# Combining the first group's tokens during the last batch, and loading weight blocks four ahead

## The chip, the cores and the metric

The kernel runs on one core of one Trainium2 chip. The time is device microseconds (us) for one launch. Before the change the median of 3 runs is 1449.72 us (1448.48 to 1450.27). One execution was also recorded by the hardware profiler; it took 1448.71 us, of which 1446.8 us are the span of the trace.

## The reference

Eight batches of 576 tokens with 512 channels go through three layers in a row:

```
x  = q_s @ (k_s^T @ v)          per head (8 heads of 64); q_s: softmax over the head's channels,
                                k_s: softmax over the tokens
h  = gelu(x @ w_in);  u, v = the two halves of h (512 each)
x  = x + (u * (w_sg @ layernorm(v) + b_sg)) @ w_out
u  = x + (x^T @ U @ V)^T        rank 32, over the tokens
out = u + relu(u @ w_ch1) @ w_ch2        w_ch1 is 512 x 2048, w_ch2 is 2048 x 512
```

The large weights arrive as float64, and everything must be accurate to about single precision, so that each product is made of three: every operand is split into a high and a low part (names end in h and l), and high*high, high*low and low*high are added.

## The kernel before

**Batches.** The loop over b = 0..7 (line 1049) does one batch at a time. Its stages on TensorE are Vh (`emit_Vh`, tile pv: the v half of x @ w_in, then layer norm), Uh (`emit_Uh`, tile pu: the u half, four pieces f), S (`emit_S`, tile pS: the product with w_sg, four pieces f, then `split_G`, which makes gh on ScalarE and gl on VectorE), y (`emit_y`, tile py: the product with w_out; every py adds over all four gh and gl). What is left of batch b (`emit_yT`, `emit_U`, `emit_PV`: the rank-32 layer, result yt stored to u2d in DRAM) is done during Vh of batch b + 1. Beside a batch's products the attention of the next batch is prepared (q and k in softmax, tiles qt, kt). pu, pS, py and others share three PSUM buffers, so that a product can begin when the one three earlier was read out; a pu is read out by ScalarE's `ut<-pu` (line 616).

**Steps.** The last layer works on the tokens of all batches in 5 groups of 480 (the last of 384) columns, by a scheme that needs 7 products where 8 blocks would be multiplied. Per group there are 28 steps for w_ch1 and 28 for w_ch2; a step s is 12 matmuls. It needs combinations of token blocks (`u_prep`: 11 VectorE operations and 7 ScalarE copies uh for each of two halves kc, 22 and 14 in all) and a combination of weight blocks, wd, which `fetch` reads from DRAM into a ring of five tiles wu. Group 0 is the tokens of batches 0 and 1, whose u2d has long been written when the last batch runs. Steps 0 to 6 are interleaved with the end of the last batch (line 1166); steps 7 and on run in the loop of line 1209.

**Conversions.** wd is made from the float64 weights by pieces in the queue `pieces`: 16 sets, each of 4 `Block` pieces (load stg, clamp on VectorE, exponent f on ScalarE, two bit operations on VectorE) and 7 `Factor` pieces (sometimes an add f<-f,f, a copy chw on ScalarE, its low part on GpSimd, a store wd<-chw to DRAM). `more(n)` pushes n pieces one stage further; the table `spread` says how many at each place of a batch, and every step calls `more(3)`. At most three pieces are in `loaded`, so a load is issued at most three rounds before VectorE's clamp asks for it. A chw tile has three buffers; a buffer is free when its store has landed.

**Order of the work.** TensorE runs in the order in which the program is written. In batches 0 to 6 VectorE does too, in batch 7 ScalarE, and from step 7 on ScalarE, VectorE, GpSimd and SyncE; where an engine isn't held, a list scheduler orders it when the kernel is built. All loads and stores but the token loads of u_prep and the residuals are issued by SyncE, one after another: one that waits holds up those behind it.

Of the kernel before, what the change touches and what calls it, by code (L numbers as in the profile page):

```python
# [22 lines left out]
def fused_kernel(tc, q, k, v, w_in, g_ln, w_sgT, b_sg, w_out, U, V, w_ch1, w_ch2, outT):  # L23
    nc = tc.nc
    B, S, C = q.shape
    P = 128
# [57 lines left out]
    wi_p, close_wi = opened("wi_p", side="left")  # L84
# [19 lines left out]
    wi_h = wi_p.tile([P, NC, 2 * F], F32R, name="wi_h")  # L104
    wi_l = wi_p.tile([P, NC, 2 * F], F32R, name="wi_l")
# [208 lines left out]
    class Factor(Conv):  # L314
# [12 lines left out]
        def merge(self):  # L327
# [10 lines left out]
            self.hl = stgp.tile([P, 2, CW], F32R, tag="chw", name="chw")  # L338
# [215 lines left out]
    def emit_Vh(b, t):  # L554
        xh, xl, xr, _ = x_t[b]
        pv = ps2.tile([P, 1024], F32, tag="big", name="pv")[:, 0:F]
        cols = slice(F, 2 * F)
        for kc in range(NC):
            if t < NT:
                a, l = xh[:, kc, t * P : (t + 1) * P], xl[:, kc, t * P : (t + 1) * P]  # L560
                mm(pv, a, wi_h[:, kc, cols], kc == 0, False)
                mm(pv, a, wi_l[:, kc, cols], False, False)
                mm(pv, l, wi_h[:, kc, cols], False, kc == NC - 1)
            else:
                a = xr[:, kc].rearrange("p j r -> p (j r)")
                mm(pv, a, wi_h[:, kc, cols], kc == 0, False)
                mm(pv, a, wi_l[:, kc, cols], False, kc == NC - 1)
# [40 lines left out]
    def emit_Uh(b, f):  # L608
# [5 lines left out]
        for kc in range(NC):  # L614
            prod(pu, wi_h[:, kc, fs], wi_l[:, kc, fs], xh[:, kc], xl[:, kc], kc == 0, kc == NC - 1)
# [359 lines left out]
    mid = ((0, 0, 1, 0, 1), (0, 0, 0, 1), (1, 1, 1, 1), (1, 1, 1, 1))  # L975
# [310 lines left out]
```

## Time and profile before

| | |
|---|---|
| median of 3 runs | 1449.72 us |
| profiled execution | 1448.71 us |
| its span | 1446.8 us |
| TensorE busy | 1314.5 us (91%) |
| VectorE, ScalarE, GpSimd busy | 1058.1, 605.7, 479.4 us |
| mean granted TensorE clock | 0.97 |

Batches 1 to 6 take the same time each. Batch 7 follows from 568.3 us, step 7 begins at 697.6, step 28 at 777.5. A slice of the page's second part is 36.2 us long, so the last batch and the first 28 steps are the slices 16 to 22, counted from 1.

### The profile page before, as it was taken

The numbers are of one execution on the slowest core, as the hardware profiler recorded it, in microseconds if no ns is written. First come the engines' busy times: TensorE is split into PE (matmuls) and PEld (weight loads), VectorE is DVE, ScalarE is ACT, GpSimd is POOL, SyncE is SP. The second block draws the span as 40 slices with busy tenths as digits, with TensorE's granted clock in tenths as the row PEclk, the third lists the DMA queues.
The fourth block names the chain that finished last, engine by engine and source line by source line (L and its number), as shares of the span: only waits on it lengthen the run. The fifth ranks groups of instructions, "written<-read, shape, count | busy, mean of one in ns | idle before, by whom it ended". The sixth has DMA issues, their size and how long they took to land.

```text
span 1446.8 us, 20595 instructions
## 1 busy us (share of the span) xinstructions
PE 1314.5 (91%) x7576; PEld 1156.8 (80%) x7576; DVE 1058.1 (73%) x1489; ACT 605.7 (42%) x969; POOL 479.4 (33%) x516
## 2 busy tenths in 40 slices
PE   4689999999999999938868899999999999999998
PEld 3478898989898989827757788878887888779988
DVE  7778878787878786576657894698549864986594
ACT  4665747575756564433224341134113411242132
POOL 5953626262626262642332130023101210131013
PEclk9899999999999999958988999999999999999999
DMA  7515242424242420447987777668766876688776
GB/s 239 159 35 158 99 114 99 114 98 114 99 114 99 113 99 30 165 139 239 305 287 271 249 251 230 202 230 268 235 203 198 295 240 203 206 259 283 254 239 207
DMA packets 116339, 269.16 MB, mean 186 GB/s; under 512 B 11856, under 2 KB 39312, under 8 KB 116240
## 3 DMA queue, kind: packets, MB, share of 16 engines
q1 hardware_dynamic: 108816, 239.54, 50.9%
q0 software_dynamic: 7424, 28.32, 5.8%
q8 instruction: 60, 0.98, 0.3%
q14 instruction: 39, 0.32, 0.1%
HBM read 219.58 MB, written 48.23 MB: 185 GB/s over the span
## 4 chain that ended last, share of the span: by engine, by line
PE 49%; DVE 26%; ACT 10%; DMA 7%; issue 6%; POOL 2%; SPq 1%; ACTq 0%; POOLq 0%; DVEq 0%
PE mm L49 32%; PE py L49 7%; PE pS L49 3%; DVE h L787 3%; DMA stg<-in_w_ch_dram 2%; DVE ol L787 2%; DVE f L177 2%; PE pv L49 2%; DVE ol L52 2%; DMA wd<-chw 2%; DVE qt L52 2%; DVE km L52 2%; DVE f L178 1%; DVE ul L52 1%; DVE bst L581 1%
## 5 line engine op out<-in xcount | busy, mean ns | idle before, releaser
L49 PE MATMUL mm<-oh,wu 128*128 128x480 f32 (+1 forms) x1120 | 326.7, 373 | 8.6 <-ACT oh L58 5.9
L49 PE MATMUL mm<-uh,wu 128*128 128x480 f32 (+1 forms) x1064 | 315.4, 378 | 15.1 <-DVE h L52 9.7
L49 PEld LDWEIGHTS mm<-oh,wu 128*128 128x128 f32 x1120 | 207.9, 188 | 40.3 <-ACT oh L58 12.7
L49 PEld LDWEIGHTS mm<-uh,wu 128*128 128x128 f32 x1064 | 202.0, 192 | 44.9 <-DVE h L52 11.0
L49 PE MATMUL mm<-ol,wu 128*128 128x480 f32 (+1 forms) x560 | 211.8, 378 | 11.7 <-DVE ol L52 9.3
L49 PE MATMUL mm<-ul,wu 128*128 128x480 f32 (+1 forms) x532 | 200.9, 378 | 0.0
L52 POOL TENSOR_TENSOR res<-res,u 128x960 f32<-128x960 f32 (+1 forms) x20 | 53.6, 2681 | 375.5 <-ACT u L58 311.8
L52 DVE TENSOR_TENSOR h<-mm,u 128x960 f32<-128x960 f32 (+1 forms) x76 | 84.5, 1112 | 87.9 <-PE mm L49 87.9
L49 PEld LDWEIGHTS mm<-ol,wu 128*128 128x128 f32 x560 | 105.4, 188 | 35.7 <-DVE ol L52 18.3
L52 POOL TENSOR_TENSOR chw<-f,chw 128x256 fp32r<-128x256 f32 x112 | 90.3, 813 | 130.4 <-ACT chw L58 129.2
L916 ACT ACTIVATE h<-h 128x960 f32<-128x960 f32 (+1 forms) x20 | 19.5, 974 | 261.2 <-DVE h L52 261.2
L52 DVE TENSOR_TENSOR u<-mm,u 128x960 f32<-128x960 f32 (+1 forms) x72 | 80.0, 1111 | 46.2 <-PE mm L49 46.1
L49 PEld LDWEIGHTS mm<-ul,wu 128*128 128x128 f32 x532 | 102.1, 192 | 13.0
L896 POOL DMA_DIRECT2D out_dram<-res x44 | 31.9, 727 | 167.6 <-DVE res L52 167.6
L787 DVE SCALAR_TENSOR_TENSOR ol<-h,oh 128x960 fp32r<-128x960 f32 (+1 forms) x60 | 74.4, 1242 | 14.5 <-ACT oh L809 14.4
L58 ACT ACTIVATE chw<-f 128x256 fp32r<-128x256 f32 x112 | 44.8, 410 | 88.7 <-DMA wd<-chw 40.7
L49 PE MATMUL py<-gh,wo_h 128*128 128x288 f32 x256 | 59.4, 314 | 20.9 <-ACT gh L58 18.5
L755 ACT ACTIVATE uh<-ust 128x480 fp32r<-128x480 f32 (+1 forms) x70 | 38.2, 580 | 83.1 <-DVE ust L52 76.9
L52 DVE TENSOR_TENSOR ul<-ust,uh 128x480 fp32r<-128x480 f32 (+1 forms) x60 | 62.2, 1067 | 14.0 <-ACT uh L755 14.0
L49 PE MATMUL py<-gl,wo_h 128*128 128x288 f32 x256 | 57.0, 305 | 5.5 <-DVE gl L52 5.5
L49 PEld LDWEIGHTS py<-gh,wo_h 128*128 128x128 f32 x256 | 42.5, 197 | 23.5 <-ACT gh L58 19.4
L49 PE MATMUL pS<-sg_h,vh 128*128 128x288 f32 x256 | 55.1, 297 | 6.7 <-ACT ut L616 6.7
(171 smaller groups left out, 2990.9 us busy)
## 6 DMA issues: line engine op xcount, KB each, us to landing
wu<-wd SPq DMA_DIRECT2D x280, 512.0 KB, 4.2
wd<-chw SPq DMA_DIRECT2D x112, 256.0 KB, 2.2
stg<-in_w_ch_dram SPq DMA_DIRECT2D x64, 256.0 KB, 3.2
u2d<-yt SPq DMA_DIRECT2D x32, 288.0 KB, 2.4
vt<-in_v_dram SPq DMA_DIRECT2D x32, 256.0 KB, 6.4
ust<-u2d POOLq DMA_DIRECT2D x16, 480.0 KB, 7.1
res<-u2d POOLq DMA_DIRECT2D x16, 480.0 KB, 6.1
qt<-in_q_dram SPq DMA_DIRECT2D x7, 1024.0 KB, 6.0
```

The source lines that it names most:

```text
L49: pe.matmul(out, lhsT, rhs, start=first, stop=last)
L52: return eng.tensor_tensor(out=out, in0=a, in1=b, op=op)
L58: return act.activation(out, src, AF.Copy)
L177: dve.tensor_scalar(out=b, in0=b, scalar1=3, scalar2=None, op0=ALU.logical_shift_left)
L178: dve.scalar_tensor_tensor(out=b, in0=w[:, :, 0], scalar=29, in1=b, op0=ALU.logical_shift_right, op1=ALU.bitwise_or)
L581: dve.bn_stats(out=bst[0:n], in_=ge[0:n])
L755: act.activation(hi, t, AF.Copy, scale=-1.0 if neg else 1.0)
L787: dve.scalar_tensor_tensor(out=out, in0=a, scalar=0.0, in1=b, op0=ALU.max, op1=op)
L896: pool.dma_start(outT[2 * mh : 2 * mh + 2, :, o : o + e - t].rearrange("c p t -> p c t"), r[:, :, t - starts[g] : e - starts[g]],)
L916: act.activation(h, h, AF.Relu)
```

## The change

1. **Token combinations of the first group.** `u_prep(0)` began in S of batch 7, seven pieces of it after each S, with one staging tile for its loads (issued by GpSimd), so that the second half was loaded when the first was done. Now it begins before Uh. The first half is loaded by SyncE in four pieces into three ge tiles of the layer norm and the tile of pst; it is combined between the four Uh. The second half is loaded by GpSimd at the end of Uh and combined between the four S. For this w_in is held in two pools, u half and v half, so that the room of the v half is free when Vh is done.
2. **Loads four ahead.** When only w_ch pieces are left in `loaded`, `more` issues the loads of coming blocks until four blocks are loaded and not yet merged.
3. **Spread.** The middle batches do 13 rounds instead of 11, all in S and y; the last batch 10 instead of 5 in Vh, 12 in Uh as before, 12 instead of 8 in S, 13 instead of 12 in y. Each step calls `more(2)` instead of `more(3)`.
4. From S of batch 7 on chw tiles alternate between the three old buffers and two new ones.

```diff
-    wi_p, close_wi = opened("wi_p", side="left")
+    wiu_p, close_wiu = opened("wiu_p", side="left")
+    wiv_p, close_wiv = opened("wiv_p", side="left")
...
+    chw = [(stgp,), 0]
     class Block(Conv):
...
+        def load(self):
+            Conv.load(self)
+            Block.live += 1
         def merge(self):
             self.keep[self.a] = from_f64(self.w, self.t)
+            Block.live -= 1
...
-            self.hl = stgp.tile([P, 2, CW], F32R, tag="chw", name="chw")
+            chw[1] += 1
+            self.hl = chw[0][chw[1] % len(chw[0])].tile([P, 2, CW], F32R, tag="chw", name="chw")
...
+    def u_load_parts(g, kc):
+        n, t0 = GROUPS[g], starts[g]
+        parts = [tmpp.tile([P, F], F32, tag="ge", name="us", bufs=3) for _ in range(3)]
+        parts.append(wrk.tile([P, F], F32, tag="pst", name="us3"))
+        parts = [t[:, 0:n] for t in parts]
+        for x, t in enumerate(parts):
+            sp.dma_start(t, u2d[x % 2, kc + 2 * (x // 2), :, t0 : t0 + n])
+        return parts
...
                     if not loaded[-1].loaded:
                         loaded[-1].load()
+                if all(isinstance(x, (Block, Factor)) for x in loaded):
+                    for x in pieces:
+                        if Block.live == 4:
+                            break
+                        if not x.loaded:
+                            x.load()
...
-    mid = ((0, 0, 1, 0, 1), (0, 0, 0, 1), (1, 1, 1, 1), (1, 1, 1, 1))
+    mid = ((0, 0, 0, 0, 0), (0, 0, 0, 0), (0, 2, 3, 3), (2, 2, 1, 0))
...
         if nxt:
             k_max(nxt)
+        else:
+            close_wiv()
+            closers = []
...
+            pool2("uc", side="right")
+            first = []
+            prep = u_prep(0, (u_load_parts, lambda *x: u_load(first[0], 1)(*x)))
         for f in range(NF):
...
+            if not nxt:
+                for _ in range((0, 4, 4, 3)[f]):
+                    next(prep)
             emit_Uh(b, f)
             if f == 0:
                 emit_ln(b, NT)
...
+                else:
+                    next(prep)
...
         if not nxt:
-            close_wi()
-            closers = []
...
-            pool2("uc", side="right")
-            first, close_first = opened("first", side="left")
-            prep = u_prep(0, first, 1)
+            close_wiu()
+            pool2("chx", 2, side="right")
+            chw[0] = (stgp, p2["chx"])
+            first_p, close_first = opened("first", side="right")
+            first.append(first_p)
         for f in range(NF):
+            if not nxt:
+                for _ in range((1, 4, 4, 3)[f]):
+                    next(prep)
             emit_S(b, f)
-            if not nxt:
-                for _ in range(7):
-                    next(prep, None)
...
-                more(3)
+                more(2)
```

ScalarE in batch 7, from the end of the Uh on. uh are the copies of `u_prep` (ust and us its loaded tokens), gh the first input of py, ut the reading out of a Uh, chw and f the conversions. Before:

```order
L755 ACTIVATE uh_6851<-ust 128x480
L755 ACTIVATE uh_6853<-ust 128x480
L755 ACTIVATE uh_6859<-ust 128x480
L58 ACTIVATE chw<-f_6759 128x256
L58 ACTIVATE chw<-f_6729 128x256
L755 ACTIVATE uh_6855<-ust 128x480
L755 ACTIVATE uh_6857<-ust 128x480
L755 ACTIVATE uh_6861<-ust 128x480
L755 ACTIVATE uh_6863<-ust 128x480
L755 ACTIVATE uh_6851<-ust 128x480
L755 ACTIVATE uh_6853<-ust 128x480
L58 ACTIVATE gh<-gt 128x576
```

After, from the first Uh's end on:

```order
L173 ACTIVATE f_6788<-stg 128x256
L58 ACTIVATE chw<-f_6788 128x256
L785 ACTIVATE uh_6800<-us 128x480
L785 ACTIVATE uh_6802<-us 128x480
L628 ACTIVATE ut<-pu 128x576
L58 ACTIVATE chw<-f_6667 128x256
L58 ACTIVATE chw<-f_6788 128x256
L58 ACTIVATE chw<-f_6705 128x256
L785 ACTIVATE uh_6808<-us 128x480
L785 ACTIVATE uh_6804<-us 128x480
L785 ACTIVATE uh_6806<-us 128x480
L628 ACTIVATE ut<-pu 128x576
```

Nine uh copies stood ahead of the first gh and none ahead of a ut; now five of the first half's seven stand between the ut of the Uh.

SyncE from step 7 on (wu is the weight tile of a step, stg a block to convert, wd a finished combination). Before:

```order
L727 DMA wu<-wd_1_4_72 128x1024
L196 DMA stg<-in_w_ch_dram 128x512
L343 DMA wd_1_5_99<-chw 128x512
L196 DMA stg<-in_w_ch_dram 128x512
L343 DMA wd_1_2_96<-chw 128x512
L196 DMA stg<-in_w_ch_dram 128x512
L343 DMA wd_1_6_97<-chw 128x512
L727 DMA wu<-wd_1_3_73 128x1024
L343 DMA wd_1_7_98<-chw 128x512
L343 DMA wd_1_3_101<-chw 128x512
L727 DMA wu<-wd_2_1_74 128x1024
L727 DMA wu<-wd_2_2_75 128x1024
```

After:

```order
L739 DMA wu<-wd_1_4_72 128x1024
L355 DMA wd_2_7_105<-chw 128x512
L198 DMA stg<-in_w_ch_dram 128x512
L355 DMA wd_2_3_108<-chw 128x512
L739 DMA wu<-wd_1_3_73 128x1024
L198 DMA stg<-in_w_ch_dram 128x512 x2
L739 DMA wu<-wd_2_1_74 128x1024
L198 DMA stg<-in_w_ch_dram 128x512
L739 DMA wu<-wd_2_2_75 128x1024
L355 DMA wd_2_4_107<-chw 128x512
L355 DMA wd_2_1_102<-chw 128x512
```

A load was followed by the store of a factor of the set before, as pieces came up; now the loads of the next set stand together, and fewer transfers lie between two wu.

ScalarE in Uh of a middle batch (qt and kt are the exponentials for the next batch, ACT_TABLE_LOAD changes the function table, ut reads a Uh out). Before:

```order
L427 ACT_TABLE_LOAD
L427 ACTIVATE qt<-qt 128x512
L427 ACTIVATE qt<-qt 64x512
L410 ACTIVATE kt<-kt 128x512
L58 ACTIVATE chw<-f_4028 128x256
L410 ACTIVATE kt<-kt 128x512
L58 ACTIVATE chw<-f_3823 128x256
L410 ACTIVATE kt<-kt 128x512
L58 ACTIVATE chw<-f_3780 128x256
L616 ACT_TABLE_LOAD
L616 ACTIVATE ut<-pu 128x576
```

After:

```order
L439 ACT_TABLE_LOAD
L439 ACTIVATE qt<-qt 128x512
L439 ACTIVATE qt<-qt 64x512
L422 ACTIVATE kt<-kt 128x512 x3
L628 ACT_TABLE_LOAD
L628 ACTIVATE ut<-pu 128x576
```

The three chw copies ahead of the last table load and ut are gone from there; they stand in S and y.

## Rows read from the trace of the kernel before

**Rows 1.** The page, the span in 40 equal slices: TensorE busy, TensorE clock

```profile
PE   4689999999999999938868899999999999999998
...
PEclk9899999999999999958988999999999999999999
```

**Rows 2.** Busy time by stretch, columns in the first row; x counts instructions

```profile
core 0: us, PE busy (x) PEld busy (x) DVE busy (x) ACT busy (x) POOL busy (x), PEclk, DMA share, GB/s
601.60:616.20 14.60, 14.60 (x110) 14.39 (x108) 7.42 (x11) 3.83 (x9) 9.93 (x11) 1.00 0.63 198
616.20:660.20 44.00, 19.97 (x98) 17.87 (x98) 27.32 (x43) 14.39 (x33) 16.55 (x19) 0.61 0.47 160
660.20:697.60 37.40, 27.78 (x121) 22.04 (x120) 27.59 (x53) 12.12 (x29) 10.50 (x14) 0.91 0.78 255
697.60:777.50 79.90, 65.34 (x253) 53.37 (x253) 48.04 (x90) 26.96 (x61) 26.63 (x36) 0.87 0.85 293
868.10:904.25 36.15, 36.15 (x168) 31.06 (x167) 15.49 (x15) 3.95 (x4) 1.08 (x2) 1.00 0.71 231
```

**Rows 3.** Instructions in order of time, TensorE; in brackets idle time before, releaser

```profile
629.64 0.85 PE L49 MATMUL py<-gh,wo_h 128*128 128x288 f32 x2 [13.41 <-ACT gh L58]
...
637.37 0.85 PE L49 MATMUL py<-gh,wo_h 128*128 128x288 f32 x2 [5.04 <-ACT gh L58]
```

**Rows 4.** Chain of waits, start and length in us

```profile
603.81 6.91 DMA wd<-chw
...
623.82 4.56 DMA ust<-u2d
```

**Rows 5.** Who waited for whom, ScalarE, 588 to 660; us in total, times, longest

```profile
ACT chw L58 <- DMA wd<-chw: 14.3, 4, 5.2
```

**Rows 6.** Instructions in order of time, VectorE

```profile
613.14 1.16 DVE L52 TENSOR_TENSOR ul<-ust,uh 128x480 fp32r<-128x480 f32 x1
...
639.35 0.65 DVE L52 TENSOR_TENSOR ul<-ust,uh 128x480 fp32r<-128x480 f32 x1
...
645.93 1.28 DVE L52 TENSOR_TENSOR gl<-gt,gh 128x576 fp32r<-128x576 f32 x1
```

**Rows 7.** Who waited for whom, TensorE, 660.2 to 697.6

```profile
PE pw L49 <- DVE pst L52: 3.0, 1, 3.0
PE pt L670 <- DVE yl L52: 2.2, 1, 2.2
```

**Rows 8.** Who waited for whom, TensorE, 697.6 to 777.5

```profile
PE mm L49 <- DVE h L52: 9.7, 3, 4.7
PE mm L49 <- DVE u L52: 1.7, 1, 1.7
```

**Rows 9.** Who waited for whom, VectorE, 697.6 to 777.5

```profile
DVE stg L165 <- DMA stg<-in_w_ch_dram: 16.9, 10, 3.5
DVE f L52 <- POOL chw L52: 10.9, 9, 2.2
```

**Rows 10.** Transfers, 697.6 to 777.5: sum; issues with KB each, us to landing

```profile
DMA packets 10447, 23.38 MB, mean 293 GB/s; under 512 B 1133, under 2 KB 1646, under 8 KB 10442
...
wd<-chw SPq DMA_DIRECT2D x35, 256.0 KB, 4.2
stg<-in_w_ch_dram SPq DMA_DIRECT2D x16, 256.0 KB, 5.8
```

**Rows 11.** Who waited for whom, TensorE, batches 1 to 6 (132 to 568.3)

```profile
PE pS L49 <- ACT ut L616: 6.7, 6, 1.7
```

**Rows 12.** Chain of waits, batch 2, start and length in us

```profile
244.42 0.31 ACT chw L58
...
246.40 1.28 ACT L616
```

**Rows 13.** Busy time by stretch, y of batch 2; columns as in rows 2

```profile
264.30:270.30 6.00, 6.00 (x46) 5.76 (x45) 3.74 (x7) 1.72 (x4) 1.25 (x1) 1.00 0.01 3
```

**Rows 14.** Transfers, 204.3 to 276.4: issues with KB each, us to landing

```profile
wd<-chw SPq DMA_DIRECT2D x7, 256.0 KB, 2.0
```

More of the change, by code (lines that the diff above doesn't have):

```diff
@@ L102, in fused_kernel @@
     bb = cst.tile([P, S], F32, name="bb")
-    wi_h = wi_p.tile([P, NC, 2 * F], F32R, name="wi_h")
-    wi_l = wi_p.tile([P, NC, 2 * F], F32R, name="wi_l")
+    wi = [
+        tuple(p.tile([P, NC, F], F32R, name=f"wi{x}{i}") for x in "hl") for i, p in enumerate((wiu_p, wiv_p))
+    ]
     wo_h = wo_p.tile([P, NF, C], F32R, name="wo_h")
@@ L279, in fused_kernel, with conv_cols @@
     stores = deque()
-    def conv_cols(src, hi, lo, cols, eng):
+    def conv_cols(src, hi, lo, c, eng, off=0):
         for kc in range(NC):
-            h, l = hi[:, kc, cols], lo[:, kc, cols]
-            yield Conv(src[kc * P : (kc + 1) * P, cols], lambda h=h, l=l: (h, l), eng)
+            h, l = hi[:, kc, c : c + CW], lo[:, kc, c : c + CW]
+            yield Conv(src[kc * P : (kc + 1) * P, off + c : off + c + CW], lambda h=h, l=l: (h, l), eng)
     def conv_w_in(c, eng):
-        return conv_cols(w_in, wi_h, wi_l, slice(c, c + CW), eng)
+        part = c // F
+        return conv_cols(w_in, *wi[part], c - part * F, eng, part * F)
     def conv_w_out(c, eng):
-        return conv_cols(w_out, wo_h, wo_l, slice(c, c + CW), eng)
+        return conv_cols(w_out, wo_h, wo_l, c, eng)
     def conv_uv(eng):
@@ L731, in fused_kernel, with u_load, load @@
     uc = {}
-    def u_prep(g, pl, bufs, eng=dve, raw=dve):
-        n, t0 = GROUPS[g], starts[g]
-        def load(kc):
+    def u_load(pl, bufs):
+        def load(g, kc):
+            n, t0 = GROUPS[g], starts[g]
             u = pl.tile([P, 2, 2, NM], F32, tag="ust", name="ust", bufs=bufs)
@@ L740, in load, with u_prep @@
                 pool.dma_start(u[:, h, :, 0:n], u2d[:, kc + 2 * h, :, t0 : t0 + n].rearrange("j p n -> p j n"))
-            return u
-        loads = [load(kc) for kc in range(bufs)]
+            return [u[:, h, j, 0:n] for h in range(2) for j in range(2)]
+        return load
+    def u_load_parts(g, kc):
+        n, t0 = GROUPS[g], starts[g]
+        parts = [tmpp.tile([P, F], F32, tag="ge", name="us", bufs=3) for _ in range(3)]
[4 more added lines that the diff above has]
+        return parts
+    def u_prep(g, load, eng=dve, raw=dve):
+        n = GROUPS[g]
+        blocks = [load[0](g, 0)]
+        if load[0] is load[1]:
+            blocks.append(load[1](g, 1))
         yield
@@ L749, in u_prep @@
         for kc in range(2):
-            u = loads[kc] if kc < bufs else load(kc)
-            u11, u12, u21, u22 = (u[:, h, j, 0:n] for h in range(2) for j in range(2))
+            if kc == len(blocks):
+                blocks.append(load[1](g, 1))
+                yield
+            u11, u12, u21, u22 = blocks[kc]
             def split(a, t, e, neg=False):
@@ L1086, in fused_kernel, with pool2 @@
             k_max(nxt)
+        else:
+            close_wiv()
+            closers = []
+            def pool2(key, *args, **kw):
+                p2[key], close = opened(key, *args, **kw)
+                closers.append(close)
+            pool2("uc", side="right")
+            first = []
+            prep = u_prep(0, (u_load_parts, lambda *x: u_load(first[0], 1)(*x)))
         for f in range(NF):
@@ L1213, in fused_kernel @@
         if pieces or loaded or bounded or begun or merged or stores:
-            more(3)
+            more(2)
             if not (pieces or loaded or bounded or begun or merged or stores):
@@ L1235, in fused_kernel @@
                 if j == 0:
-                    prep = u_prep(g + 1, p2["ust"], 2)
+                    prep = u_prep(g + 1, (ust_load, ust_load))
                     next(prep)
```

22 lines of the change are left out of this document (10 added, 12 removed).

## The prediction

> **What bounds the kernel now.** I read the 40 slices first: TensorE is at 9 tenths or more in nearly all of them and falls in slices 18 to 22, where its clock falls too [rows 1]. That is the last batch's end and the steps of the first group. Cut into stages, full speed is to be seen in 868.1 to 904.25: 168 matmuls in 36.15 us, 0.215 us each, so a step of 12 costs 2.58 us [rows 2]. Steps 7 to 27 are 21 steps, 54.2 us at that speed, and take 79.9 us (697.6 to 777.5), so 25.7 us are lost there; the DMA engines are 85% busy in them [rows 2]. Worst is 616.2 to 660.2: 44.0 us with TensorE busy for 19.97 at a mean clock of 0.61, most of it the 96 matmuls of py [rows 2]. There the first py waits 13.41 us for gh and a later one 5.04 us [rows 3], and the last gl ends at 645.93 + 1.28 = 647.2 us [rows 6]. What delays gh is, in the chain of waits, first a store of a weight combination (6.91 us, where in a middle batch one lands in 2.0 [rows 4, 14]), on which ScalarE's chw copies wait 14.3 us in all, 5.2 at the most [rows 5], then u_prep itself with its second load (4.56 us, [rows 4]). In the middle batches the largest wait of TensorE is pS for ut, 6.7 us over six batches [rows 11].
>
> **The change part by part.** Every term is what the profiled execution, 1448.71 us (span 1446.8 and 1.9 around it), would lose or gain.
>
> Token combinations. Nothing is computed less: 22 VectorE operations and 14 copies, which ran in S and after it, move into Uh and S. They fill idle VectorE time: of the 14.60 us from 601.6 to 616.2 it was busy for 7.42, so 7.2 are free [rows 2]; and the second load no longer waits for the first half, so its 4.56 us lie beside other work [rows 4]. Together 11.8: the last gl comes 12 us earlier, and the end of py with it. More than the two waits for gh, 13.41 + 5.04 = 18.4 us, can hardly be won [rows 3]. What is late next is VectorE again: the second half's eleven operations still stand between the gl of the four f. The other bound is a loss: ScalarE, in program order here, now has uh and chw copies ahead of each ut, with S waiting for ut's buffer. If a chw waits for its store as long as once before, 5.2 us, S starts that much later [rows 5]. VectorE's list behind it hides it as long as gl and not pS ends last; so I count nothing, with 5.2 as price. The four new loads stand in SyncE's queue among the stg loads and the u2d stores; the store of the last pst and the layer norm's GpSimd operations release their tiles, and behind them wait only conversions. The new pools cost no instruction; that ring tiles wait for u_prep's last tile is hidden by py, four times 24 matmuls.
>
> At this place a rule speaks against the change. The same ul operation takes 1.16 us at 613.14 and 0.65 at 639.35 [rows 6]; the first stood beside GpSimd work, the second didn't. The eleven operations of the second half were of the fast kind and now come beside chw and gt on GpSimd, so up to 11 * 0.51 = 5.6 us of the 12 may go. The Trainium skill, SBUF — State Buffer, "Who interferes with whom", states it as a rule: a VectorE instruction with two inputs in SBUF contends with a GpSimd instruction that reads SBUF, and the one that comes second is blocked until the first is done. By that rule the last gl comes only 6.4 us earlier; the trace agrees as to the two durations. I keep 12, since both kinds of ul are in it, and give the rule a rival.
>
> Steps 7 to 27. Two things change. Fewer pieces: after step 7's fetch SyncE had 51 loads and stores of the conversions (16 and 35 [rows 10]) and, counted in the new order, has 33. 18 transfers of 262,144 bytes are 4.72 of the 23.38 MB, which at the mean of 293 GB/s are 16.1 us [rows 10]. And loads come earlier: a load takes 5.8 us to land [rows 10], with three pieces per step it was issued about a step before its clamp, and VectorE, in program order, stood 16.9 us on it [rows 9]; behind the clamp stood the h and u additions on which TensorE waited 9.7 + 1.7 = 11.4 us [rows 8]. With four blocks ahead and two rounds per step a load has about three steps, some 8 us. The rest of the 25.7 us is clock: busy 65.34 against 54.2 us is 11.1 us at a mean clock of 0.87 [rows 2], which falls where TensorE has stood still. Bounds: 0 (the stage keeps its pace, only with less to move) and 25.7 (all of it). I take 14, a little under 16.1, since VectorE's adds also stand 10.9 us on GpSimd's chw [rows 9], which remain, though with five chw buffers instead of three.
>
> Steps 0 to 6 and the rank-32 layer (660.2 to 697.6). 21 rounds become 14. TensorE waits here for VectorE's pst (3.0) and yl (2.2, [rows 7]), which stand behind conversions; VectorE is busy for 27.59 of 37.40 us [rows 2]. If all that were conversions, a third, 9.2 us, would go; nothing at the least. I take 4, near the middle. Eight factor adds go from VectorE to GpSimd, since more factors are made before the switch at step 0; that is in it.
>
> Middle batches. Three chw copies of 0.31 us lie ahead of the table load and the ut for which pS waits [rows 12]; without them ut is up to 0.93 us earlier, 5.6 in six batches, of the 6.7 [rows 11]. In return S and y get all 13 rounds, two more than all stages had. From 264.3 to 270.3 GpSimd is busy for 1.25 and VectorE for 3.74 of 6.00 us, with the DMA engines at 0.01 [rows 13], which covers them; if a gh or gl came late there, the six batches could lose as much as they can win. Between -5.6 and 5.6 I take a gain of 3, by the copies' row. Vh of the last batch gets five rounds more; no row shows its cover, its price is the same kind of wait and lies in the bounds of the token term.
>
> Sum: 3 + 12 + 4 + 14 = 33 us, 1448.71 - 33 = 1415.7. The median of the runs shown is 1.0 above the profiled execution: 1417.
>
> **The rivals.**
> - Last gl no earlier: ScalarE's queue (chw behind their stores, uh behind their loads) now delays ut, pS and gh, and what VectorE gains in Uh it loses in S. For it: the 6.91 us store fell in S, where the DMA engines were at 63% [rows 2] and the second half's loads come now. Against it: the first half's loads leave that place. The 12 us are gone: 1429.
> - Blocked by GpSimd: half of the 12, by the 0.51 us above: 1417 + 5.6 = 1423.
> - Steps no faster: the stage is at 85% DMA share [rows 2], and loads in bunches of four with stores between them let wu land late, so that TensorE waits for wu instead of h. Against it: 18 transfers less and a ring of five. The 14 us are gone: 1431. With the first rival too: 1443.
> - Slower: in y of the middle batches a set's seven chw use three buffers in turn. With a copy of 0.31 [rows 12], twice that for GpSimd's part (an estimate from that row) and a store of 2.0 us [rows 14], seven take 2.9 * 7 / 3 = 6.9 us of about 12, two stretches like that of rows 13. With a store of 6.91 [rows 4] they take 18.3, ScalarE and GpSimd reach the next batch's xh and xl 6.3 us late, and six batches lose 38: 1417 + 3 + 38 = 1458. It outweighs the sum from 6 us a batch, a store of 6.8. Against it: the idle DMA engines there [rows 13].
> - More: stages 7 to 27 and py reach full speed, 25.7 and 18.4 instead of 14 and 12: 1417 - 18 = 1399.
>
> **How the numbers follow.** Forecast 0.44, GpSimd 0.12, gl no earlier 0.13, steps no faster 0.13, both 0.06, slower 0.06, more 0.06. Range 1400 to 1436: it leaves out both, slower and most of more. 0.2% of 1449.72 is 2.9 us, about what a measurement of this kernel can tell from no change; only the slower rival and a tail of "both" reach above 1446.8. Faster 0.91, the same 0.02, slower 0.07.
>
> **What would show it.** Right: from the last pS to the last gl are about 19 us, where they were 31 (616.2 to 647.2); the first py waits under 5 us for gh; TensorE's mean clock over py is near 1; from the first mm of step 7 to the first oh are about 66 us; VectorE's wait of clamps on stg falls from 16.9 to a few us; pS waits for ut under 4 us in batches 1 to 6. Wrong: a new wait of pS on ut in the last batch of more than 5 us; a wait of mm on wu in steps 7 to 27 of more than 8; a middle batch longer than before, or a wait of pv on xl in it.

## The result, and the profile after

| | before | after |
|---|---|---|
| median of the runs timed together | 1449.1 us (4 runs) | 1402.68 us (4 runs, 1399.94 to 1404.85) |
| ratio, 95% interval | 1 | 0.9683 (0.9655 to 0.9711) |
| span of the profiled execution | 1446.8 us | 1398.1 us |
| mean granted TensorE clock | 0.97 | 0.986 |

The change saves 46.4 us; 32.7 were forecast (1449.72 - 1417). The profiled execution is the fastest of the four, 2.7 us under their median; its span is 48.7 us shorter. Cut where the same matmul starts in both traces, the 48.7 us fall as follows. A stage begins with its first matmul; Uh, S and py are one stretch, since waits only move between S and py. A difference of 0.1 is rounding.

| stretch | before | after | saved | forecast |
|---|---|---|---|---|
| start to Vh of batch 7 | 568.1 | 565.3 | 2.8 | 3 |
| Vh of batch 7 | 20.1 | 20.0 | 0.1 | 0 |
| Uh of batch 7 to step 0 | 71.8 | 64.5 | 7.3 | 12 |
| steps 0 to 6 and rank 32 | 37.6 | 29.6 | 8.0 | 4 |
| steps 7 to 27 | 79.9 | 55.1 | 24.7 | 14 |
| step 28 to the end | 669.3 | 663.6 | 5.7 | 0 |

The page's 40 slices show the place: the hole of [rows 1] is now two slices wide.

```profile
PE   4679999999999999967999999999999999999998
PEclk9889999999999999988999999999999999999999
```

Busy time by stretch, with the columns of [rows 2]: Uh, S, y, steps 0 to 6, steps 7 to 27.

```profile
585.30:598.70 13.40, 13.05 (x96) 12.82 (x96) 7.78 (x19) 6.24 (x12) 4.37 (x6) 1.00 0.71 229
598.70:619.17 20.47, 16.78 (x112) 16.54 (x113) 17.42 (x24) 10.11 (x25) 15.54 (x18) 0.92 0.56 182
619.17:649.80 30.63, 17.35 (x98) 15.97 (x97) 23.40 (x38) 9.89 (x24) 17.07 (x19) 0.72 0.61 217
649.80:679.40 29.60, 24.84 (x123) 20.46 (x121) 23.49 (x44) 10.20 (x26) 8.28 (x12) 1.00 0.90 307
679.40:734.50 55.10, 55.09 (x252) 47.39 (x253) 46.12 (x72) 21.36 (x46) 19.10 (x26) 1.00 1.00 364
```

In the last row TensorE never stands still, 55.09 of 55.10 us at full clock, with the DMA engines at a share of 1.00 and 364 GB/s. Before, it was busy for 65.34 of 79.90 us at a clock of 0.87, with the DMA engines at 0.85 and 293 GB/s [rows 2]. S has become longer, 20.5 for 14.6 us, at a clock of 0.92; y is shorter by 13.4. TensorE's longer waits, in order of time:

```profile
599.49 0.53 PE L49 MATMUL pS<-sg_h,vh 128*128 128x288 f32 x2 [1.13 <-ACT ut L628]
606.37 0.53 PE L49 MATMUL pS<-sg_h,vh 128*128 128x288 f32 x2 [2.90 <-ACT ut L628]
...
623.95 0.54 PE L49 MATMUL py<-gl,wo_h 128*128 128x288 f32 x2 [4.34 <-DVE gl L52]
...
630.03 0.85 PE L49 MATMUL py<-gh,wo_h 128*128 128x288 f32 x2 [5.17 <-ACT gh L58]
```

The two waits for ut are new. ScalarE's instructions in order of time say why:

```profile
592.63 0.65 ACT L628 ACTIVATE ut<-pu 128x576 f32<-128x576 f32 x1 [3.45 <-DMA u2d<-yt]
...
598.29 0.60 ACT L785 ACTIVATE uh<-us 128x480 fp32r<-128x480 f32 x1 [0.94 <-DMA us<-u2d]
598.80 0.63 ACT L628 ACTIVATE ut<-pu 128x576 f32<-128x576 f32 x1
...
604.68 1.10 ACT L785 ACTIVATE uh<-us 128x480 fp32r<-128x480 f32 x2 [3.61 <-DVE us L52]
605.68 0.63 ACT L628 ACTIVATE ut<-pu 128x576 f32<-128x576 f32 x1
```

Uh ends at 598.7, but the third ut is made at 605.68, right behind two uh that stood 3.61 us on VectorE's combinations. ScalarE is held to program order in this batch, so a copy of the combinations that is late holds up the reading out of PSUM behind it, and with it the next pS. In the trace all seven uh of the first half stand ahead of the last ut, two more than the five counted above from the order of the program.

In steps 7 to 27 the two waits of VectorE in [rows 9] were 16.9 and 10.9 us. After, no wait on stg is left in the list of this stage, and of the others 5.0 us of ScalarE's on a store, 3.3 of VectorE's on chw and 0.7 of TensorE's on h:

```profile
ACT chw L58 <- DMA wd<-chw: 5.0, 1, 5.0
DVE f L52 <- POOL chw L52: 3.3, 3, 2.2
...
PE mm L49 <- DVE h L52: 0.7, 1, 0.7
```

### The profile page after: what moved, and what is told of

Read it like the earlier page. It is cut to its first block, busy times and chain, and to the rows that moved or that the text cites. A ratio compares the mean times of both kernels' runs of the same rounds, so it can differ in the third digit from the quotient of the medians.

```text
span 1398.1 us, 20610 instructions
## 1 busy us (share of the span) xinstructions
PE 1298.7 (93%) x7576; PEld 1150.5 (82%) x7576; DVE 1049.2 (75%) x1481; ACT 605.0 (43%) x969; POOL 487.9 (35%) x522
## 4 chain that ended last, share of the span: by engine, by line
PE 54%; DVE 23%; ACT 7%; issue 7%; POOL 5%; DMA 5%; SPq 0%; ACTq 0%; DVEq 0%; POOLq 0%
PE mm L49 37%; PE pv L49 6%; PE py L49 4%; DVE h L817 3%; DVE ol L52 2%; DVE ol L817 2%; PE px L49 2%; POOL qt L52 2%; DMA stg<-in_w_ch_dram 1%; DVE t L817 1%; DVE f L179 1%; DVE qt L52 1%; PE pp L49 1%; DVE gl L52 1%; DVE ul L52 1%
## 5 line engine op out<-in xcount | busy, mean ns | idle before, releaser
L49 PE MATMUL mm<-uh,wu 128*128 128x480 f32 (+1 forms) x1064 | 308.4, 371 | 0.7 <-DVE h L52 0.7
L49 PEld LDWEIGHTS mm<-uh,wu 128*128 128x128 f32 x1064 | 198.1, 188 | 27.2 <-DVE h L52 1.0
L49 PE MATMUL mm<-ul,wu 128*128 128x480 f32 (+1 forms) x532 | 198.1, 372 | 0.0
L52 POOL TENSOR_TENSOR res<-res,u 128x960 f32<-128x960 f32 (+1 forms) x20 | 58.6, 2928 | 377.0 <-ACT u L58 312.1
L52 DVE TENSOR_TENSOR u<-mm,u 128x960 f32<-128x960 f32 (+1 forms) x72 | 80.0, 1111 | 48.7 <-PE mm L49 48.6
L817 DVE SCALAR_TENSOR_TENSOR ol<-h,oh 128x960 fp32r<-128x960 f32 (+1 forms) x60 | 72.4, 1208 | 11.4 <-ACT oh L839 11.2
L49 PE MATMUL py<-gh,wo_h 128*128 128x288 f32 x256 | 59.0, 313 | 14.4 <-ACT gh L58 5.2
L785 ACT ACTIVATE uh<-ust 128x480 fp32r<-128x480 f32 (+1 forms) x63 | 34.2, 578 | 70.4 <-DVE ust L52 70.4
L52 DVE TENSOR_TENSOR ul<-ust,uh 128x480 fp32r<-128x480 f32 (+1 forms) x54 | 58.3, 1111 | 7.8 <-ACT uh L785 7.8
L52 POOL TENSOR_TENSOR vl<-ge,vh 128x512 fp32r<-128x512 f32 x32 | 46.0, 1439 | 35.8 <-ACT vh L58 35.7
```

The source lines that it names most:

```text
L49: pe.matmul(out, lhsT, rhs, start=first, stop=last)
L52: return eng.tensor_tensor(out=out, in0=a, in1=b, op=op)
L785: act.activation(hi, t, AF.Copy, scale=-1.0 if neg else 1.0)
L817: dve.scalar_tensor_tensor(out=out, in0=a, scalar=0.0, in1=b, op0=ALU.max, op1=op)
```

## The experiments

Twelve kernels: four take one part out of the changed kernel, three put one part into the kernel before, five try other tables of rounds. This table has the stages of all, from the profiled execution of each, and the ratio to runs of the kernel before on the same chip, with its 95% interval. "Middle" is Vh of batch 1 to Vh of batch 7, "Uh, S, y" ends with step 0, "oh" is the start of the first oh on ScalarE.

| kernel | middle | Uh, S, y | steps 0–6 | steps 7–27 | oh to end | ratio |
|---|---|---|---|---|---|---|
| before | 433.7 | 71.8 | 37.6 | 79.9 | 671.6 | 1 |
| after | 431.5 | 64.5 | 29.6 | 55.1 | 671.0 | 0.9683 (0.9655–0.9711) |
| no_ahead | 431.1 | 64.7 | 30.2 | 57.2 | 670.7 | 0.9705 (0.9688–0.9722) |
| old_spread | 433.5 | 65.9 | 30.6 | 72.1 | 671.6 | 0.9833 (0.9815–0.985) |
| prep_old | 431.5 | 68.2 | 29.0 | 55.1 | 671.6 | 0.9698 (0.9679–0.9718) |
| no_chx | 431.1 | 63.4 | 33.3 | 59.0 | 671.3 | 0.9756 (0.9741–0.977) |
| before_mid | 422.5 | 70.7 | 37.8 | 78.8 | 670.9 | 0.992 (0.9903–0.9937) |
| prep_only | 433.9 | 65.4 | 32.5 | 81.7 | 671.1 | 0.9918 (0.9902–0.9935) |
| before_chx | 433.9 | 71.3 | 29.6 | 76.8 | 673.9 | 0.9892 (0.9877–0.9907) |
| steps3 | 431.5 | 64.8 | 30.9 | 65.6 | 678.4 | 0.9761 (0.9745–0.9776) |
| mid_shift | 432.9 | 64.1 | 31.4 | 55.1 | 673.3 | 0.9694 (0.9678–0.9709) |
| mid11_s3 | 423.2 | 65.2 | 34.5 | 69.5 | 678.9 | 0.9729 (0.9711–0.9746) |
| mid11_mix | 423.2 | 63.9 | 38.2 | 56.7 | 671.1 | 0.9684 (0.9669–0.9698) |
| mid11_last | 423.2 | 67.9 | 33.3 | 55.1 | 671.2 | 0.9674 (0.966–0.9689) |

**no_ahead** takes the loads four ahead out of the changed kernel.

```
-                if all(isinstance(x, (Block, Factor)) for x in loaded):
-                    for x in pieces:
-                        if Block.live == 4:
-                            break
-                        if not x.loaded:
-                            x.load()
```

> The changed kernel without the loads four ahead; everything else is kept (two pieces a step, 35 conversion transfers left after the twelfth weight fetch, 33 with the loads ahead and 51 before). Theory L (early loads): VectorE, in program order, stood 16.9 us on loads in steps 7 to 27 before, and the loads ahead took that away; without them the wait of clamps on stg is at least 10 us there, the stretch from the first mm of step 7 to the first oh is 68 to 78 us instead of 55, and the time is 1417 to 1428. Rival F (fewer pieces): the stretch runs at full rate because less is left to convert; without the loads ahead it takes 55 to 61 us, and the time is 1402 to 1409.

1406.87 us (ratio 0.9705), steps 7 to 27 in 57.2 us. The wait on loads did come back, as theory L said, but TensorE hardly felt it. VectorE's wait in steps 7 to 27:

```profile
DVE stg L167 <- DMA stg<-in_w_ch_dram: 11.7, 8, 2.5
```

So 11.7 us of VectorE's idle time cost TensorE 2 us there, and the first oh 6. Rival F's time came: with the new table VectorE has most of that time to spare. The ratio's interval overlaps the changed kernel's; taking the loads ahead out costs about 3 us by the ratios, not clear of the noise.

**old_spread** puts the old tables back and keeps the loads, the early combinations and the five chw buffers.

```
-    mid = ((0, 0, 0, 0, 0), (0, 0, 0, 0), (0, 2, 3, 3), (2, 2, 1, 0))
+    mid = ((0, 0, 1, 0, 1), (0, 0, 0, 1), (1, 1, 1, 1), (1, 1, 1, 1))
-    spread[B - 1] = ((2, 2, 2, 2, 2), (3, 3, 3, 3), (3, 3, 3, 3), (4, 3, 3, 3))
+    spread[B - 1] = ((1, 1, 1, 1, 1), (3, 3, 3, 3), (2, 2, 2, 2), (3, 3, 3, 3))
...
-                more(2)
+                more(3)
```

> The changed kernel with the old tables: the middle batches 11 rounds at the old places, the last batch 5, 12, 8, 12, and three pieces a step; loads four ahead, early token combinations and five chw buffers stay. 47 conversion transfers are left after the twelfth weight fetch. Theory L: clamps wait under 5 us on stg in steps 7 to 27 and the stretch to the first oh stays under 60 us; lost are the 3 us of the middle batches and most of the 8 us of steps 0 to 6: 1411 to 1418. Rival F: the stretch goes back to 72 to 80 us, and the time is 1430 to 1440.

1425.15 us, between the two. Steps 7 to 27 take 72.1 us, 17.0 more than with the new table, at the lower end of rival F. Steps 0 to 6 take only 30.6 us although each of them makes three rounds again: fewer rounds, to which the prediction put down their gain, aren't needed for it. What TensorE waits for in steps 7 to 27 is another thing than before, its own weight tiles:

```profile
PE mm L49 <- DMA wu<-wd: 4.1, 6, 1.2
PE mm L49 <- DVE u L52: 3.0, 2, 2.0
PE mm L49 <- DVE h L52: 2.6, 2, 1.6
```

**prep_old** puts the token combinations back to where they were, after each S.

```
-            prep = u_prep(0, (u_load_parts, lambda *x: u_load(first[0], 1)(*x)))
...
+            prep = u_prep(0, (u_load(first_p, 1), u_load(first_p, 1)))
...
             emit_S(b, f)
+            if not nxt:
+                for _ in range(7):
+                    next(prep, None)
```

> The changed kernel with the token combinations of the first group at their old place, seven pieces after each S, both halves loaded by GpSimd into one tile. Theory T (the early combinations won the 7.5 us between the start of S and step 0): TensorE's wait of pS on ut (4.0 us) goes, S takes 14.6 us, py waits 18 us or more for gh and gl, and the time is 1408 to 1418. Rival V: VectorE's whole list of Uh, S and y ends when it ends, and the place of the combinations in it decides little; S gains 6 us and y loses as much: 1400 to 1406.

1405.27 us, 0.9698: as rival V said, within the noise of the changed kernel. S loses its waits for ut, and py waits as before the change. TensorE from Uh to step 0:

```profile
PE py L49 <- ACT gh L58: 20.2, 3, 12.3
PE py L49 <- DVE gl L52: 2.0, 1, 2.0
```

Together 22.2 us of waits, against 17.3 in the changed kernel (8.1 for gl, 5.2 for gh, 4.0 for ut).

**prep_only** is the counterpart: the first part of the change alone in the kernel before (old tables, three chw buffers, no loads ahead).

```
+            pool2("uc", side="right")
+            first = []
+            prep = u_prep(0, (u_load_parts, lambda *x: u_load(first[0], 1)(*x)))
...
+            if not nxt:
+                for _ in range((0, 4, 4, 3)[f]):
+                    next(prep)
             emit_Uh(b, f)
```

> The kernel before with the first part of the change alone: token combinations of the first group from Uh on, with the two pools of w_in; no loads ahead, three chw buffers, the old rounds, three pieces a step. Theory T (the term of 12 us as it was predicted): the last gl ends 12 us earlier and the time is 1436 to 1441. Theory V (what the undoing of it showed: with or without it the last gl hangs on VectorE's whole list, and 2.6 us are lost with the old place): pS waits for ut, the last gl comes at most 5 us earlier, 1444 to 1451.

1438.59 us, 0.9918: 12 us faster, theory T's number, though not by theory T's way. Stretches Uh to step 0, and steps 0 to 6:

```profile
588.87:654.25 65.38, 48.91 (x304) 46.35 (x305) 38.20 (x66) 25.97 (x58) 32.14 (x37) 0.79 0.55 185
654.25:686.80 32.55, 26.90 (x124) 22.45 (x122) 26.04 (x52) 11.64 (x29) 10.69 (x14) 0.90 0.83 268
```

6.4 us come before step 0 (65.4 for 71.8) and 5.1 in steps 0 to 6 (32.5 for 37.6). The last gl ends at 642.1, 5.1 us earlier than before the change, not 12. In the changed kernel steps 0 to 6 are quick without it too, 29.0 us in prep_old; by before_chx, next, the buffers suffice for that. This fits with the small loss when the combinations are put back there.

**no_chx** leaves out the two further chw buffers, **before_chx** puts these alone into the kernel before.

```
-            pool2("chx", 2, side="right")
-            chw[0] = (stgp, p2["chx"])
```

> The changed kernel with the three old chw buffers to the end; all else is kept. Theory X (the two further buffers are what quickened steps 0 to 6, since that stage took 29.6 to 30.6 us in every kernel that has them, whatever its pieces per step, its loads or the place of the combinations, and 37.4 to 37.8 in both that have not): the stage from step 0 to step 7 takes 34 to 38 us, ScalarE's chw copies wait over 20 us for their stores from the start of S to the first oh, against some 14 now, and the time is 1410 to 1420. Rival F (fewer pieces per step did it): the stage takes 29 to 32 us, and the time is 1402 to 1407.

> The kernel before with the two further chw buffers from S of the last batch on, and nothing else. Theory X (leaving them out of the changed kernel cost 11.6 us and brought back 44.2 us of waits of chw copies for their stores): chw waits for stores fall from 40.7 us to under 20 between S and the first oh, and the time is 1436 to 1444. Rival: with three pieces a step and loads only three pieces ahead VectorE is held by loads anyhow (16.9 us), so that the buffers win 0 to 4 us: 1446 to 1451.

1414.24 us (0.9756) without them, 1434.88 us (0.9892) with them alone: by the ratios 10.6 us lost, 15.6 us won. Theory X holds in both directions as to the waits and the sign of the time; its sizes were off a little, with steps 0 to 6 at 33.3 us in no_chx instead of 34 to 38, and before_chx 1 us quicker than its range. ScalarE's chw copies waiting for the store that frees their buffer, from S to the first oh, in no_chx:

```profile
ACT chw L58 <- DMA wd<-chw: 44.2, 21, 5.6
```

and in before_chx:

```profile
ACT chw L58 <- DMA wd<-chw: 18.4, 5, 6.3
```

In the kernel before, and in the changed kernel:

```profile
ACT chw L58 <- DMA wd<-chw: 40.7, 21, 5.6
...
ACT chw L58 <- DMA wd<-chw: 13.9, 4, 5.3
```

The steps 0 to 6 of before_chx run like those of the changed kernel, with nothing else changed (the second row is steps 7 to 27):

```profile
658.70:688.30 29.60, 24.91 (x123) 20.35 (x122) 25.86 (x47) 11.66 (x30) 10.28 (x14) 1.00 0.90 295
688.30:765.05 76.75, 62.72 (x252) 49.77 (x253) 51.17 (x94) 27.45 (x60) 25.94 (x36) 0.93 0.91 312
```

**before_mid** moves the eleven rounds of a middle batch of the kernel before to S and y, with no round added.

```
-    mid = ((0, 0, 1, 0, 1), (0, 0, 0, 1), (1, 1, 1, 1), (1, 1, 1, 1))
+    mid = ((0, 0, 0, 0, 0), (0, 0, 0, 0), (0, 2, 3, 2), (2, 1, 1, 0))
```

> The kernel before with one edit: the eleven rounds of the middle batches stand in S and y only ((0,2,3,2) and (2,1,1,0)), none in Vh and Uh. Theory (the term of 3 us for the middle batches): pS waits for ut under 2 us in batches 1 to 6 instead of 6.7, and the time falls by 2 to 4 us against the kernel before, 1445 to 1447. Rival: the waits only move, to py on ql and px; the time is that of the kernel before within 1.5 us.

1438.57 us, 0.992: 11.5 us faster, three times the upper end of what I expected, though the waits did go as the theory said. Batches 1 to 5 are 70.2 us long instead of 72.2. In the changed kernel the six batches are only 2.2 us shorter than before; it has two rounds more in S and y, and with eleven rounds (mid11_s3 and the two after it, below) they are as short as here. TensorE's waits over the six batches, in the kernel before, besides those of pS in [rows 11]:

```profile
PE pw L49 <- DVE yt L52: 3.5, 6, 0.6
PE pv L49 <- ACT ge L571: 1.3, 6, 0.2
```

before_mid:

```profile
PE pv L49 <- ACT ge L571: 1.3, 6, 0.2
PE py L49 <- DVE ql L52: 1.1, 1, 1.1
```

and the changed kernel:

```profile
PE py L49 <- DVE ql L52: 3.7, 5, 1.0
PE py L49 <- DVE yt L52: 2.6, 2, 1.4
PE pv L49 <- ACT ge L583: 1.3, 6, 0.2
PE pS L49 <- ACT ut L628: 0.7, 2, 0.5
```

pw on yt is gone in both, and of pS on ut, 6.7 us in [rows 11], at most 0.7 is left; what the changed kernel gives back are the waits of py. VectorE in batch 1 of the changed kernel, in order of time, shows how:

```profile
186.88 0.83 DVE L167 TENSOR_SCALAR stg<-stg 128x256 f32<-128x256 f32 x1
188.76 1.60 DVE L52 TENSOR_TENSOR ql<-pt,qh 128x576 fp32r<-128x576 f32 x2 [1.05 <-ACT qh L58]
...
192.46 1.54 DVE L180 SCALAR_TENSOR_TENSOR f<-stg,f 128x256 uint32<-128x256 uint32 x1
194.03 0.76 DVE L52 TENSOR_TENSOR yt<-py,x 128x576 f32<-128x576 f32 x1
```

and ScalarE:

```profile
187.74 0.44 ACT L173 ACTIVATE f<-stg 128x256 f32<-128x256 f32 x1 [1.57 <-DVE stg L167]
188.08 0.64 ACT L58 ACTIVATE qh<-pt 128x576 fp32r<-128x576 f32 x1
```

The py of this batch waits 0.59 us for ql and 1.17 for yt. The ql isn't held by VectorE's list: VectorE stands idle for 1.05 us until qh is there, and qh stands on ScalarE behind the exponent f of a conversion, which had waited 1.57 us for the clamp (0.83 us beside GpSimd work, 0.28 to 0.30 alone). The yt stands right behind a merge of 1.54 us (0.40 to 0.43 alone), beside a GpSimd operation from 192.44 to 193.72.

**steps3** keeps everything and makes three rounds a step.

```
-                more(2)
+                more(3)
```

(at both places where steps call it)

> The changed kernel with three pieces a step instead of two, at all steps from 0 on; all else is kept. 28 conversion transfers are left after the twelfth weight fetch instead of 33, and the last is issued before the 22nd fetch instead of the 31st. Theory R (the work per step was too much: with three pieces a step VectorE reaches the h and u additions late): from the first mm of step 7 to the first oh 62 us or more, TensorE waits over 5 us for h and u there, 1409 to 1420. Rival W (the work that is left is what counts, not how it is spread over steps; done sooner it also leaves VectorE earlier to the first oh): 53 to 57 us, 1398 to 1405.

1414.92 us, 0.9761. Theory R's time and stage (65.6 us), but not its cause: VectorE does get to the first oh early, 51.0 us after step 7 begins, and TensorE's wait for h is 2.9 us. TensorE in steps 7 to 27:

```profile
PE mm L49 <- DMA wu<-wd: 6.3, 4, 2.7
PE mm L49 <- DVE h L52: 2.9, 2, 1.8
```

The weight tiles come late. 28 transfers of the conversions are left after the twelfth fetch, fewer than the changed kernel's 33, but they are issued within ten steps instead of nineteen, and stand in SyncE's queue between the fetches. The bytes of the stage (19.86 MB, 20.03 in the changed kernel) and the work that is left can't explain the loss; how much falls on one step can. That the queue is the way by which it acts is argued from the waits, not shown.

**mid_shift** shifts the thirteen rounds within S and y of a middle batch.

```
-    mid = ((0, 0, 0, 0, 0), (0, 0, 0, 0), (0, 2, 3, 3), (2, 2, 1, 0))
+    mid = ((0, 0, 0, 0, 0), (0, 0, 0, 0), (1, 2, 3, 2), (2, 1, 1, 1))
```

> The changed kernel with the thirteen rounds of a middle batch shifted: (1,2,3,2) in S and (2,1,1,1) in y instead of (0,2,3,3) and (2,2,1,0); all else is kept. Theory: the eleven rounds in S and y alone made a middle batch 70.2 us long, and the thirteen 71.9 on average since the third round of the last S and the second of y put clamps and shifts of VectorE ahead of ql and yt, on which py waits; with one round each moved to the first S and the last y these waits (py on ql and yt 6.3 us in all) go, and the time falls by 5 to 10 us, 1393 to 1398. Rival: thirteen rounds don't fit into S and y of a batch; the waits only move, to pS on ut or pv on ge, and the time stays at 1400 to 1405.

1405.48 us, 0.9694: no difference that can be measured. py still waits 3.6 us for yt and 3.4 for ql over the six batches; the middle takes 432.9 us. My theory on the places of these two rounds falls; thirteen rounds are too many there.

**mid11_s3**, **mid11_mix** and **mid11_last** take the eleven rounds of before_mid into the changed kernel and make the missing twelve elsewhere: by three rounds at every step; by three rounds in steps 0 to 6 and five more in Vh and y of the last batch; by twelve more in the last batch.

All three:

```
-    mid = ((0, 0, 0, 0, 0), (0, 0, 0, 0), (0, 2, 3, 3), (2, 2, 1, 0))
+    mid = ((0, 0, 0, 0, 0), (0, 0, 0, 0), (0, 2, 3, 2), (2, 1, 1, 0))
```

The last batch in mid11_mix, and in mid11_last:

```
-    spread[B - 1] = ((2, 2, 2, 2, 2), (3, 3, 3, 3), (3, 3, 3, 3), (4, 3, 3, 3))
+    spread[B - 1] = ((3, 3, 2, 2, 2), (3, 3, 3, 3), (3, 3, 3, 3), (4, 4, 4, 4))
```

```
-    spread[B - 1] = ((2, 2, 2, 2, 2), (3, 3, 3, 3), (3, 3, 3, 3), (4, 3, 3, 3))
+    spread[B - 1] = ((3, 3, 3, 3, 3), (4, 4, 4, 4), (3, 3, 3, 3), (4, 4, 4, 4))
```

> The changed kernel with the eleven rounds of a middle batch of (0,2,3,2) and (2,1,1,0), and three pieces a step to take up what is left. 37 conversion transfers are left after the twelfth weight fetch. If middle batches of 70.2 us and quick steps add up: 8 us less in the middle batches, and by theory W no loss after them, 1392 to 1398. By theory R, or if the twelve rounds that came into the steps cost what those of the old tables cost (17 us for fourteen transfers), the steps lose 8 to 17 us, and the time is 1402 to 1412.

> The changed kernel with eleven rounds in a middle batch ((0,2,3,2) and (2,1,1,0)) and the twelve that are missing done later: two more in Vh and three more in y of the last batch, and three pieces instead of two in steps 0 to 6, two from step 7 on (34 transfers left after the twelfth weight fetch). Middle batches 70.2 us each, 8 us less in all; steps 0 to 6 cost 1 to 2 us more, as with three pieces at every step, y of the last batch 0 to 3 more, steps 7 to 27 stay at 55 us: 1396 to 1402. Rival: the rounds cost in the last batch and the steps what they saved: 1402 to 1408.

> As the kernel with eleven rounds in a middle batch, but the twelve that are missing all in the last batch: fifteen rounds in Vh, sixteen in Uh, twelve in S, sixteen in y; two pieces a step. Middle batches win 8 us; Vh of the last batch keeps TensorE at 20 us; from Uh to step 0 VectorE's list grows by seven rounds of some 0.8 us, against 64.5 us now up to 70: 1396 to 1402. Rival: VectorE is the bound from Uh to step 0 and its clamps run at half speed or less beside GpSimd, so that the seven rounds cost 8 us or more: 1402 to 1410.

1410.04 us (0.9729), 1405.32 us (0.9684) and 1403.09 us (0.9674). The middle batches took 423.2 us in all three, 8.3 less than in the changed kernel, and all of it was paid again: in mid11_last Vh takes 3.1 us more, Uh to step 0 3.3, steps 0 to 6 3.7. In mid11_mix steps 0 to 6 take 38.2 us, 8.6 more where 1 to 2 were expected; TensorE waits there 5.8 us for ScalarE's u. So three rounds a step, which cost that stage 1.0 us in old_spread and 1.3 in steps3, aren't free in it in every schedule. Vh, Uh to step 0, and steps 0 to 6 of mid11_last:

```profile
557.80:580.90 23.10, 19.52 (x88) 14.24 (x86) 15.87 (x37) 16.80 (x33) 15.22 (x20) 1.00 0.37 128
580.90:648.80 67.90, 47.45 (x305) 45.01 (x306) 47.23 (x83) 27.99 (x65) 43.35 (x49) 0.82 0.61 207
648.80:682.00 33.20, 26.86 (x123) 21.57 (x121) 25.24 (x45) 11.06 (x28) 9.69 (x13) 0.95 0.91 314
```

Twelve rounds cost 8.3 us in the middle batches, 0.7 each, and 10.1 us in the last with its steps 0 to 6, 0.8 each. No version here beats the changed kernel by more than the measurement can tell.

## Why the prediction was right, and where it was not

The direction and the places were right; the time lies 14 us under the forecast and 2.7 inside the range. The sum of 33 should have been 48.7 for the profiled execution, and each of its four terms hides an error. Two were too small and one too large, so that the time stays inside the range partly by luck. Of the rivals, "more" (1399, chance 0.06) came nearest in time, and half of it happened: steps 7 to 27 took 55.1 us, against 54.2 at full speed, but py ran at a clock of 0.72. A slip in the slower rival, 2.9 * 7 / 3 = 6.8 and not 6.9, changes nothing.

**Steps 7 to 27, 14 us: mis-sized, and bounded wrongly.** To the start of step 28 24.7 us were won, nearly the upper bound of 25.7, and 5.7 more behind it, beyond the bound. The first oh came 47.7 us after step 7 began, where about 66 were forecast. The bound took TensorE for what ends the stage. But what follows, the preparation of the second layer's inputs, hangs on VectorE and ScalarE, and starts when they reach the first oh. The oh of ScalarE, first and last start us, before:

```profile
L809 ACT ACTIVATE oh<-h x60: 825/990/997, 775.2 to 1431.5; 128x960 fp32r<-128x960 f32 x48, 128x768 fp32r<-128x768 f32 x12
```

and after:

```profile
L839 ACT ACTIVATE oh<-h x60: 829/990/1000, 727.2 to 1382.9; 128x960 fp32r<-128x960 f32 x48, 128x768 fp32r<-128x768 f32 x12
```

From the first to the last oh it is 656.3 and 655.7 us: all but 0.6 of the 48.7 us is won before the first oh. Before, TensorE reached step 28 2.3 us after the first oh had begun and waited 0.66 us for its ol; now it comes 7.4 us after, so that VectorE has a lead of 5 us where it is the slower one. The column "oh to end" shows it for the others: 670.7 to 673.9 us, save where TensorE comes 15 or 16 us late (steps3, mid11_s3). The term's two reasons fared unlike each other. The loads ahead, which I had put beside the bytes as a cause, are worth about 3 us (no_ahead). The bytes, 18 transfers at 293 GB/s, gave 16.1 us, and undoing the tables cost 17.0 in this stage; but the agreement is luck, since steps3 has still fewer transfers left and loses 10.5 us. With five chw buffers and three pieces a step the stage takes 65.6, 69.5, 72.1 and 76.8 us at 28, 37, 47 and 51 transfers left (steps3, mid11_s3, old_spread, before_chx); with two pieces it takes 55.1, 56.7 and 57.2 at 33, 34 and 35 (after, mid11_mix, no_ahead). So of the 17.0 us some 10.5 go with the pieces per step and the rest with what is left, as an estimate, since these kernels differ in other parts too.

**Steps 0 to 6, 4 us: won 8.0, and for another reason.** I put it on fewer rounds. old_spread, with 21 rounds again, has 30.6 us; before_chx, with nothing but two more chw buffers, 29.6. The buffers aren't the only way to it: prep_only, with 21 rounds and three buffers, has 32.5, and no_chx, with 14 and three, 33.3, so that the gains overlap. The further buffers were in the prediction only as a remark beside the steps 7 to 27; of the three parts run alone they won most, 15.6 us, and taken out they cost 10.6. Taking out the tables costs more, 21.7 (old_spread); these weren't run alone as a whole. The rows for the buffers were there: ScalarE's chw copies waited 14.3 us for their stores up to step 0 [rows 5], and it is 40.7 us in 21 waits up to the first oh. I read these waits as a delay of gh and not as what holds up VectorE behind them. How the buffers reach VectorE is shown only in part: with the buffers alone its waits from step 0 to the first oh fall from 20.4 to 14.0 us on loads and from 14.4 to 12.1 on GpSimd's chw.

**Token combinations, 12 us: won 7.3, with the loss that I had priced and not counted.** "S waiting for ut's buffer" and "5.2 as price" stand in the text; the wait came, 4.0 us and 1.8 us more with the clock at 0.92 in S, through uh and not through chw. The last gl ended at 637.2, 18.0 us after the last pS (31.0 before; about 19 were forecast). So 13.0 us were won on this side; but the last pS had itself become 5.9 us later, counted from the first pu, and the last gl came 7.1 us earlier instead of 12. The step that failed is the price left out of the sum: VectorE's list didn't hide it. The mean clock over py is 0.72 and not near 1; py still waits 4.34, 5.17 and 2.87 us. The rule of the Trainium skill, SBUF — State Buffer, "Who interferes with whom", that I weighed there bore out in part: the combinations on VectorE took 20.1 us in all, 17.7 before (the groups of ul, us and ust, 22 operations each), 2.4 us more and not 5.6. That 7.1 us is near the 6.4 by that rule is luck, then. Alone (prep_only) the part won its 12 us, in two places of which I had seen one.

**Middle batches, 3 us: right by accident.** 2.2 us were won in the six batches. The 0.6 up to the end of batch 0, where the tables are the same, is noise: over these fourteen kernels batch 1 begins between 133.1 and 135.6. Behind the 2.2 are two large terms that cancel: the move won 11.2 us (before_mid), where I had bounded it at 5.6 from the three copies of 0.31 us, and the two further rounds gave 9.0 back, 5.2 of them as waits of py. The bound should have been the sum of all waits of TensorE in these batches that begin with ScalarE or VectorE being late, 6.7 for pS on ut, 3.5 for pw on yt and 1.3 for pv on ge, 11.5 us (the last stayed). "A middle batch longer than before" was one of the signs of a wrong mechanism, and batch 6 is, 73.7 us against 72.9, batches 1 and 2 by 0.2 and 0.3.

The parts do not add up. Alone, three of them win 11.5, 12.1 and 15.8 us of the medians, 39.4 in all; taken out singly of the changed kernel, two of these cost 2.2 and 10.6 by the ratios. A likely reason, which no run isolates: a part that relieves VectorE and ScalarE before the first oh wins only as long as these are late for it.

Not settled: why Uh to step 0 is 3.6 us shorter in prep_old than in the kernel before (68.2 against 71.8), though the combinations stand at the same place in both. 3.0 of the 3.6 lie between the last pS and the last gl (31.0 and 28.0 us). The buffers alone (before_chx, 71.3) and the middle tables alone (before_mid, 70.7) hardly do it, and the loads ahead and the last batch's table weren't run alone.

## What to carry to other kernels

Follow the longest list of an engine through to the event that the next stage begins with, and bound a gain by that event, not by TensorE standing still in one stage: a lead that is won on VectorE is paid out later. Before a schedule is changed, add up who waits for a buffer to be freed by its store; two more buffers of 2 KB a partition won more here, run alone, than moving 36 operations (15.6 and 12 us). And where work has to go somewhere, look for the stage in which it is free (two pieces a step here) instead of shifting it between stages where it costs nearly the same, 0.7 and 0.8 us a round.

## What the runs showed of the hardware

VectorE's shifts and clamps, which have one input, were stretched beside GpSimd work, as those operations with two inputs were. In the changed kernel's trace the 58 shifts of 128x256 that overlap no GpSimd operation took 0.27 to 0.30 us and the 37 such clamps 0.28 to 0.30; of the others, 30 and 27, the median is 0.61 and 0.82, and seven of each took no more than 0.35. Two of the longest, VectorE:

```profile
607.53 1.50 DVE L179 TENSOR_SCALAR f<-f 128x256 uint32<-128x256 uint32 x1
...
613.21 1.52 DVE L167 TENSOR_SCALAR stg<-stg 128x256 f32<-128x256 f32 x1
```

GpSimd at these times:

```profile
607.12 1.76 POOL L52 TENSOR_TENSOR gt<-gt,ut 128x576 f32<-128x576 f32 x1 [1.90 <-DVE gt L648]
...
612.80 1.77 POOL L52 TENSOR_TENSOR gt<-gt,ut 128x576 f32<-128x576 f32 x1 [0.50 <-DVE gt L648]
```

Each VectorE operation began within a gt of GpSimd (607.12 to 608.88, 612.80 to 614.57) and ended some 0.15 us after it. Alone these two are quicker than a merge of the same size, which has two inputs and takes 0.40 to 0.43 us, so this need not hold of every operation with one input. And the DMA engines' share of 0.85 with 293 GB/s in [rows 2] was no limit, though I held it for one in a rival: the same stage moves 364 GB/s at a share of 1.00 without TensorE waiting for a weight tile.
